# Whole-block stores with x in token order, and an earlier first cast of k, in a linear-attention and MLP kernel

## The chip, the cores and the metric

One core of a Trainium2 chip runs the whole program. The metric is the device time of one execution in microseconds; the median of several runs counts. The engines are TensorE (PE in the profile, with its weight loads as PEld), VectorE (DVE), ScalarE (ACT), GpSimd (POOL) and SyncE (SP), which here only issues transfers.

## The reference

A decayed linear attention over 4 batches, 8 heads, 768 tokens and a head size of 64, in blocks of 64 tokens with a carried state, and then an MLP with a sigmoid-approximated GELU (512 to 2048 to 512) on the 3072 tokens:

```python
for b in range(nb):
    intra = einsum('bhic,bhjc->bhij', qb, kb) * Dmask        # lam**(i-j) for i >= j
    intra = einsum('bhij,bhjd->bhid', intra, vb)
    inter = einsum('bhid,bhde->bhie', qb * lam_pow, kv_state)
    out[:, :, sl] = intra + inter
    kv_state = lam_block * kv_state + einsum('bhsd,bhse->bhde', kb * rev_pow, vb)
x = out.transpose(0, 2, 1, 3).reshape(B * S, H * D)          # 3072 x 512
h = x @ w_in
g = h * (1.0 / (1.0 + exp(-1.702 * h)))
return g @ w_out                                             # 3072 x 512, float32
```

## The kernel before

The 3072 tokens are worked in six waves of 512 (`NW` = 6, `W` = 512). A wave has an attention part, which leaves x turned, features on partitions and tokens on columns, in the tile `xT[w]` (128 x 4 x 512, bf16), and an MLP part. The attention of wave w + 1 is threaded through the MLP of wave w.

**Waves 0 and 1** (`w < ND`) take 256 successive tokens of each of two batches. Half `c` of such a wave is one batch. The loads (L84) put two successive tokens on each partition, so within a block of 128 tokens the attention works with the even tokens first and the odd ones after. `d_out` leaves two PSUM tiles for a half, and `d_x` (L328, called with `i` = 0 and 1) copies each of them, 128 x 512 in f32, to 128 columns of `xT` as bf16. Column a * 64 + s of the block is then token 2s + a. Four such copies are made in each of the two waves: in `end` by ScalarE and VectorE (L756, L757), for the first half of wave 0 both by ScalarE. The order of the columns is carried through the MLP to the partitions of the output block, so a block of 128 tokens goes out in two stores, the even tokens from partitions 0 to 63 and the odd ones from 64 to 127. For wave 1 they stand in `after_product` (L492 to L494), for wave 0 in `leave0` (L536 to L539), which keeps them in `late[n]` for SyncE to issue later (L846, L847, L855, L856). Each store carries two such blocks of tokens (`0:2`) and 256 output columns.

**Waves 2 to 5** take 128 tokens of all four batches. The loads of k, q and v (L88) come in two halves each, over batches. `do_cast` (L196) multiplies a half of k or q by powers of lam and writes bf16, in two instructions; on these waves GpSimd does it (L212). `turn_dma` (L246) then turns the half by a transposing DMA, issued by SyncE (L248). `kT` has one buffer for each half, `ks` two, the loaded `kf` and `qf` one.

**The MLP** uses a scheme of seven products in place of eight for 2 x 2 blocks in both layers. `x_sums` (L569, four VectorE instructions at L577) and `g_sums` (L436, L444) make the sums on its operand side, `in_product` (L579) the first layer's products and `product` (L451) the second's. The results pass through tiles of one pool (tag `o`, 8 buffers): `h_sb` of the first layer (L604) and `o_sb` of the output blocks (L484). Output block 2, 5, 4 and 3 of a wave follow the products of these numbers.

**The order** is written out by hand: `STEPS[w]` is a string of steps that `one_step` (L618) carries out one by one. `a` to `d` with a digit are first-layer products of the wave's groups, `A` to `D` their GELU, `P` a second-layer product, `S`, `M`, `m` the scores and masks of the next wave's attention, `R` its outputs and the state update (`n_state`, L360, VectorE at L371). `K0`, `K1`, `Q0`, `Q1` are the casts of k's and q's halves on GpSimd, `tk0` to `tq1` their turns; they work on wave w + 1. `Lk` and `Lw` load k and q two waves ahead and v one wave ahead. `X` makes the x sums of the next wave. A `+` ahead of a step counts it to the next wave. `G` is a gate: a one-element copy on GpSimd (`gate_pool`, L681) that reads the last of the x sums, so that the casts behind it begin only when these are made. Each engine carries out its instructions in order, and so does SyncE with the transfers that it issues.

Of the kernel before, what the change touches and what calls it, by code (L numbers as in the profile page):

```python
# [25 lines left out]
def kernel(  # L26
# [13 lines left out]
    nc = tc.nc  # L40
    f32 = mybir.dt.float32
    bf16 = mybir.dt.bfloat16
    B, H, S, D = q.shape
    P = 128
# [3 lines left out]
    G = W // P  # L48
# [3 lines left out]
    FFC = d_ff // P  # L52
# [62 lines left out]
    A, Z = slice(0, 64), slice(64, P)  # L115
# [78 lines left out]
    cast, trans, masked, xT, g_of, h_ps, o_ps, t_ps = {}, {}, {}, {}, {}, {}, {}, {}  # L194
# [132 lines left out]

    def d_x(w, c, i, t, copy):  # L328
        n0 = (2 * c + i) * P
        copy(xT[w][:, :, n0 : n0 + P], t)  # L330

    def n_scores(w, p):
        s2 = [acc("ps_s") for _ in range(2)]
# [65 lines left out]
    def mlp1(w, fc):  # L399
        if w not in g_of:  # L400
            g_of[w] = gp.tile([P, FFC, W], bf16, tag="g", name="g_sb")
        j, i = w_in_of[fc]
        h = acc("ps_h", shape=[P, W], tag="mm")
        for kc in range(KC):
            nc.tensor.matmul(h, w_in_sb[j][:, kc, i * P : (i + 1) * P], xT[w][:, kc, :],
                             start=(kc == 0), stop=(kc == KC - 1))
        nc.scalar.activation(g_of[w][:, fc, :], h, GELU)
# [13 lines left out]
    half_sum, blocks, part, c11, c12 = {}, {}, {}, {}, {}  # L421
# [52 lines left out]
    def after_product(w, n, bank, t):  # L474
        if n in (1, 6, 7):
            part[w, n, t.start] = op.tile([P, 2, 256], f32, tag="part", bufs=6, name="part")
            nc.scalar.copy(part[w, n, t.start][:, t], bank[:, t])
            if (w, 4, t.start) in c12:
                after_product(w, 4, c12.pop((w, 4, t.start)), t)
            return  # L480
        if n == 4 and (w, 6, t.start) not in part:
            c12[w, 4, t.start] = bank
            return
        o = op.tile([P, 2, 256], f32, tag="o", name="o_sb")  # L484
        if n == 3:
            nc.scalar.copy(o[:, t], bank[:, t])
        else:
            nc.vector.tensor_tensor(o[:, t], part[w, {2: 1, 5: 7, 4: 6}[n], t.start][:, t], bank[:, t], op=ADD)
        i, c = {2: (0, 0), 3: (0, 1), 4: (1, 0), 5: (1, 1)}[n]
        cols = slice(256 * c, 256 * c + 256)  # L490
        if w < ND:
            rows5 = out.rearrange("(b t s a) d -> a b s t d", t=S // P, s=64, a=2)  # L492
            for a, rows in enumerate((A, Z)):
                nc.sync.dma_start(out=rows5[a, 2 * w + i, :, 0:2, cols], in_=o[rows])  # L494
        else:
            nc.sync.dma_start(
                out=out.rearrange("(b s) d -> s b d", s=S)[w * P : (w + 1) * P, 2 * i + t.start : 2 * i + t.stop, cols],
                in_=o[:, t])
# [19 lines left out]
    def leave0(n):  # L518
        bank = blocks[0, BANK0[int(n)]]
        if n in (1, 6, 7):  # L520
            part[0, n] = op.tile([P, 2, 256], f32, tag="part", bufs=6, name="part")
            nc.scalar.copy(part[0, n], bank)
            return
        if n == 4.5:
            nc.gpsimd.tensor_tensor(o21[0], o21[0], part[0, 7], op=ADD)
            return
        o = op.tile([P, 2, 256], f32, tag="o", name="o_sb")
        if n == 3:
            nc.scalar.copy(o, bank)
        else:  # L530
            nc.vector.tensor_tensor(o, part[0, {2: 1, 5: 7, 4: 6}[n]], bank, op=ADD)
        if n == 4:
            o21.append(o)
        i, c = {2: (0, 0), 3: (0, 1), 4: (1, 0), 5: (1, 1)}[n]

        def store():  # L536
            rows5 = out.rearrange("(b t s a) d -> a b s t d", t=S // P, s=64, a=2)
            for a, rows in enumerate((A, Z)):
                nc.sync.dma_start(out=rows5[a, i, :, 0:2, 256 * c : 256 * c + 256], in_=o[rows])  # L539
        late[n] = store  # L540

    GR = {w: (1, 2, 0, 3) if w > 1 else (1, 2, 3) for w in range(1, NW)}
# [15 lines left out]
    def in_sums(g, which=(0, 1, 2, 3)):  # L558
        t1, t2, t3, t4 = TI[g]
        b11, b12, b21, b22 = (in_pair(g, kh, j) for kh in range(2) for j in range(2))  # L560
        ops = ((t1, b12, b11), (t2, b22, t1), (t3, b22, b12), (t4, b21, t2))
        for i in which:
            o, x, y = ops[i]
            nc.vector.tensor_tensor(o, x, y, op=SUB)

    def x_half(w, i, kh):
        return xT[w][:, 2 * kh : 2 * kh + 2, 256 * i : 256 * i + 256]

    def x_sums(w, which=(0, 1, 2, 3)):  # L569
        if w not in x_sum:  # L570
            x_sum[w] = [xp.tile([P, 2, 256], bf16, tag=f"xs{n}", bufs=1, name="x_s") for n in range(4)]
        s1, s2, s3, s4 = x_sum[w]
        a11, a12, a21, a22 = (x_half(w, i, kh) for i in range(2) for kh in range(2))
        ops = ((s3, a11, a21, SUB), (s1, a21, a22, ADD), (s2, s1, a11, SUB), (s4, a12, s2, SUB))
        for i in which:
            o, x, y, f = ops[i]
            nc.vector.tensor_tensor(o, x, y, op=f)  # L577
# [33 lines left out]
    def in_gelu(w, g, n, bank=None):  # L611
        bank = bank or h_out.pop((w, g, n))
        i, j = {2: (0, 0), 3: (0, 1), 4: (1, 0), 5: (1, 1)}[n]
        a, b = (GROUPS[g][u][j] for u in range(2))
        nc.scalar.activation(g_of[w][:, a : b + 1 : b - a, 256 * i : 256 * i + 256], bank, GELU)  # L615


    def one_step(w, s):  # L618
        if s[0] == "+":
            w, s = w + 1, s[1:]  # L620
        x, a = w + 1, s[1:]
        if s[0] == "f":
            mlp1(w, int(a))
        elif s[0] in "abcd":
            k = "abcd".index(s[0])
            in_product(w, GR[w][k], int(s[1]), TAGS[w][k], dve_copy if s[2:] == "v" else act_copy)
        elif s[0] in "ABCD":
            in_gelu(w, GR[w]["ABCD".index(s[0])], int(a))
        elif s[0] == "i":
            in_sums(0, (int(a),))  # L630
        elif s[0] == "P":
            product(w, int(s[1]), (int(s[2]),))
        elif s[0] in "kq":
            do_cast(x, int(a), s[0], nc.vector)
        elif s[0] in "KQ":
            do_cast(x, int(a), s[0].lower(), nc.gpsimd)
        elif s[0] == "t":
            turn_dma(x, int(s[2]), s[1])
        elif s[0] == "v":
            cast_v(x, int(s[1]), ((act_copy, dve_copy)[s[2:] == "v"],))  # L640
        elif s[0] == "S":
            n_scores(x, int(a))
        elif s[0] == "M":
            n_masks(x, int(a))
        elif s[0] == "m":
            n_masks(x, int(a), True)
        elif s[0] == "R":
            n_rest(x)
        elif s[0] == "o":
            c11.pop(w)()  # L650
        elif s[0] == "X":
            x_sums(x)
        elif s[0] == "G":
            gate_pool(x_sum[w][3][0:1, 0, 0:1])
        elif s[0] == "g":
            m0, m1 = {"l": (0, 4), "h": (4, 8)}[s[1]]
            g_sums(w, m0, m1, tuple(int(c) - 1 for c in s[2:]))
        elif s[0] == "L":
            load(w + (1 if a == "w" else 2), "kq" if a == "k" else "v")
        else:  # L660
            raise ValueError(s)

    STEPS = {
# [17 lines left out]
    def gate_pool(x):  # L681
        nc.gpsimd.tensor_copy(behind_q, x)  # L682
# [209 lines left out]
```

## Time and profile before

| | |
|---|---|
| median of 3 runs | 193.22 us (192.25 to 193.78) |
| the profiled execution | 193.47 us, of which the span from first to last instruction is 191.8 us |
| granted TensorE clock | 1.00 |
| busy: TensorE, VectorE, ScalarE, GpSimd | 183.5, 154.6, 130.0, 53.8 us |
| moved by DMA | 33.91 MB, a mean of 177 GB/s |

The profile is that of one execution. Busy time is the sum of the instructions' durations on an engine; that of TensorE is partly modelled. The chain is followed back from the last instruction, each step to what released it. Line numbers such as L371 are those of the kernel before.

### The profile page before, as it was taken

How to read it: one execution, taken by the hardware profiler on the slowest of the kernel's cores; microseconds unless marked ns; L12 is line 12 of the kernel's file. 1: busy time of each engine (PE TensorE's matmuls, PEld its weight loads, DVE VectorE, ACT ScalarE, POOL GpSimd, SP SyncE). 2: the span in 40 equal slices, each digit the busy share in tenths (PEclk: the TensorE clock that was granted, in tenths of full speed). 3: DMA queues.
4: the chain of work that ended last, by engine and by line, in shares of the span. 5: the costliest groups of instructions: out<-in, count | busy, mean ns of one | idle time of the engine just before them, and what ended most of it. 6: DMA issues, size and time to landing. Idle time of an engine off the chain costs nothing.

```text
span 191.8 us, 5553 instructions
## 1 busy us (share of the span) xinstructions
PE 183.5 (96%) x2291; PEld 150.7 (79%) x2293; DVE 154.6 (81%) x296; ACT 130.0 (68%) x243; POOL 53.8 (28%) x79
## 2 busy tenths in 40 slices
PE   7779999999999999999999999999999999999993
PEld 2356545898788888888888888888888888888882
DVE  1797689997687899979799879799889797889950
ACT  4858566055869976389878388877388876597711
POOL 5298200029738000096000294000393000000000
PEclk9999999999999999999999999999999999999999
DMA  5999999999996799988899756999365903300113
GB/s 154 322 241 161 199 206 206 277 291 295 258 174 139 162 228 243 241 206 135 190 244 221 228 137 140 226 249 251 104 163 121 208 4 113 109 3 0 53 57 112
DMA packets 89599, 33.91 MB, mean 177 GB/s; under 512 B 67430, under 2 KB 89446, under 8 KB 89574
## 3 DMA queue, kind: packets, MB, share of 16 engines
q1 hardware_dynamic: 84676, 28.84, 61.7%
q0 software_dynamic: 4896, 4.72, 14.9%
q8 instruction: 18, 0.29, 0.7%
q14 instruction: 7, 0.06, 0.1%
q10 hardware_dynamic: 2, 0.00, 0.0%
HBM read 27.26 MB, written 6.29 MB: 175 GB/s over the span
## 4 chain that ended last, share of the span: by engine, by line
PE 79%; DMA 12%; DVE 4%; POOL 2%; SPq 1%; issue 0%; ACT 0%; ACTq 0%
PE ps_X L464 19%; PE ps_hX L596 17%; PE ps_V L464 9%; PE ps_hV L596 9%; DMA w_out<-in_moe_w_out_dram 6%; DMA vf<-in_v_dram 6%; PE ps_Q L464 5%; PE ps_hQ L596 4%; PE ps_X L514 3%; DVE w_out_t L431 2%; PE ps_s L338 2%; PE ps_o L393 2%; PE ps_h L417 2%; DVE g_s L444 2%; POOL w_in L184 1%; PE ps_o L380 1%
## 5 line engine op out<-in xcount | busy, mean ns | idle before, releaser
L615 ACT ACTIVATE g_sb<-h_sb 128x512 bf16<-128x512 f32 x57 | 34.5, 632 | 1.2 <-DVE h_sb L604 1.2
L464 PEld LDWEIGHTS <-g_s 128*128 128x128 bf16 x320 | 30.9, 98 | 4.1
L596 PEld LDWEIGHTS <-w_in_t 128*128 128x128 bf16 x304 | 29.7, 98 | 3.6
L224 ACT COPY part<-ps_hX 128x512 f32<-128x512 f32 x34 | 19.5, 586 | 10.4 <-PE ps_hX L596 10.3
L464 PEld LDWEIGHTS <-g_sb 128*128 128x128 bf16 x240 | 22.8, 98 | 3.4
L596 PEld LDWEIGHTS <-w_in 128*128 128x128 bf16 x228 | 22.1, 98 | 2.8
L596 PE MATMUL ps_hX<-x_s,w_in_t 128*128 128x256 bf16 x152 | 22.5, 272 | 0.0
L444 DVE TENSOR_TENSOR g_s<-g_sb 128x1024 bf16<-128x1024 bf16 (+1 forms) x26 | 16.5, 646 | 5.5 <-ACT g_sb L615 5.5
L464 PE MATMUL ps_X<-w_out_t,g_s 128*128 128x256 bf16 x160 | 19.1, 273 | 0.0
L682 POOL CAST behind_q<-x_s 1x1 f32<-1x1 bf16 x4 | 0.7, 174 | 62.2 <-DVE x_s L577 62.2
L212 POOL TENSOR_TENSOR qs<-qf,q_pow 128x512 bf16<-128x512 f32 x16 | 16.3, 1040 | 0.9 <-PE ps_o L301 0.9
L212 POOL TENSOR_TENSOR ks<-kf,k_pow 128x512 bf16<-128x512 f32 x16 | 16.3, 1039 | 0.1
L604 DVE TENSOR_TENSOR h_sb<-part,ps_hX 128x512 f32<-128x512 f32 x19 | 12.9, 681 | 3.9 <-PE ps_hX L596 3.9
L221 DVE COPY part<-ps_hV 128x512 f32<-128x512 f32 x18 | 12.4, 687 | 3.2 <-PE ps_hV L596 3.2
L604 DVE TENSOR_TENSOR h_sb<-part,ps_hV 128x512 f32<-128x512 f32 x19 | 13.0, 684 | 1.0 <-PE ps_hV L596 1.0
L604 DVE TENSOR_TENSOR h_sb<-part,ps_hQ 128x512 f32<-128x512 f32 x19 | 12.9, 681 | 0.4 <-PE ps_hQ L596 0.4
L615 ACT ACTIVATE g_sb<-ps_hX 128x512 bf16<-128x512 f32 x19 | 11.1, 588 | 1.9 <-PE ps_hX L596 1.9
L347 ACT ACTIVATE sm<-ps_s,inv_pow 128x512 bf16<-128x512 f32 x16 | 10.2, 691 | 2.5 <-PE ps_s L338 2.5
L224 ACT CAST v_sb<-vf 128x1024 bf16<-128x1024 f32 (+1 forms) x12 | 10.4, 906 | 1.6 <-DMA vf<-in_v_dram 1.6
L596 PE MATMUL ps_hQ<-xT,w_in 128*128 128x256 bf16 x76 | 11.4, 273 | 0.0
L596 PE MATMUL ps_hV<-x_s,w_in_t 128*128 128x256 bf16 x76 | 11.4, 273 | 0.0
L596 PE MATMUL ps_hV<-xT,w_in_t 128*128 128x256 bf16 x76 | 11.4, 273 | 0.0
(128 smaller groups left out, 364.4 us busy)
## 6 DMA issues: line engine op xcount, KB each, us to landing
kf<-in_k_dram SPq DMA_DIRECT2D x10, 512.0 KB, 6.3
qf<-in_q_dram SPq DMA_DIRECT2D x10, 512.0 KB, 6.7
vf<-in_v_dram SPq DMA_DIRECT2D x10, 512.0 KB, 5.9
out_dram<-o_sb SPq DMA_DIRECT2D x24, 128.0 KB, 2.4
out_dram<-o_sb SPq DMA_DIRECT2D x12, 256.0 KB, 2.6
w_out<-in_moe_w_out_dram POOLq DMA_DIRECT2D x4, 512.0 KB, 14.8
kf<-in_k_dram SPq DMA_DIRECT2D x4, 256.0 KB, 3.1
qf<-in_q_dram SPq DMA_DIRECT2D x4, 256.0 KB, 4.6
```

Of the source, the lines that this page charges most:

```text
L212: eng.tensor_tensor(x.rearrange("p b (r i j d) -> p j (b r) i d", i=2, j=2, d=D)[:, j], f.rearrange("p h (a d) -> p (h a) d", a=2).rearran ...
L221: nc.vector.tensor_copy(out, in_)
L224: nc.scalar.copy(out, in_)
L338: nc.tensor.matmul(s2[h][:, b, :], kT[hs, (b % 2) * NP + p, :], qT[hs, (b % 2) * NP + p, :], start=True, stop=True)
L347: nc.scalar.activation(sm, s, COPY, scale=inv_pow[:, n : n + 1])
L393: nc.tensor.matmul(ps_o[cs, b, :], vt[:, b, 2 * p + i, :], masked[w, 2 * R + i, j][:, b, :], start=False, stop=True, skip_group_check=True)
L444: nc.vector.tensor_tensor(o, x, y, op=f)
L464: nc.tensor.matmul(bank[:, t], x[:, m, t * P : (t + 1) * P], y, start=(n in (1, 2, 7) and t == ts[0] * last and m == 0), stop=(m == FFC // ...
L514: nc.tensor.matmul(bank[:, t], x[:, m, t * P : (t + 1) * P], y, start=(n in (1, 2, 7, 4) and t == 0 and m == 0), stop=(m == FFC // 2 - 1), ...
L596: nc.tensor.matmul(bank[:, u], z[:, kc], y[:, kc], start=(n in (1, 2, 7) and u + kc == 0), stop=(kc == 1), skip_group_check=True)
L604: nc.vector.tensor_tensor(h, h_part[w, g, {2: 1, 5: 7, 4: 6}[n]], bank, op=ADD)
L615: nc.scalar.activation(g_of[w][:, a : b + 1 : b - a, 256 * i : 256 * i + 256], bank, GELU)
```

## The change

There are three edits.

`d_x` writes each PSUM tile to `xT` with the even and odd tokens interleaved, so that the columns of a block stand in token order. The destination steps over every second element; the source is read as before.

With this the output blocks of waves 0 and 1 have token p of the block on partition p, and each is stored in one transfer of 128 partitions: 256 KB in place of two times 128 KB.

In `STEPS` of waves 1, 2 and 3 the steps `K0 tk0` of the following string (the first half of k for waves 3, 4 and 5) move ahead, from behind the gate `G` to a place behind `R`, ahead of the products 5 and 3 and their stores. They get a gate of their own, `H`, which reads the last element of the fourth of the g sums. `G` stays where it was and is now followed, on GpSimd, by `K1`.

```diff
     def d_x(w, c, i, t, copy):
         n0 = (2 * c + i) * P
-        copy(xT[w][:, :, n0 : n0 + P], t)
+        copy(xT[w][:, :, n0 : n0 + P].rearrange("p r (s a) -> p r a s", a=2), t.rearrange("p r (a s) -> p r a s", a=2))
...
         if w < ND:
-            rows5 = out.rearrange("(b t s a) d -> a b s t d", t=S // P, s=64, a=2)
-            for a, rows in enumerate((A, Z)):
-                nc.sync.dma_start(out=rows5[a, 2 * w + i, :, 0:2, cols], in_=o[rows])
+            nc.sync.dma_start(out=out.rearrange("(b t s) d -> b s t d", t=S // P, s=P)[2 * w + i, :, 0:2, cols], in_=o)
...
         def store():
-            rows5 = out.rearrange("(b t s a) d -> a b s t d", t=S // P, s=64, a=2)
-            for a, rows in enumerate((A, Z)):
-                nc.sync.dma_start(out=rows5[a, i, :, 0:2, 256 * c : 256 * c + 256], in_=o[rows])
+            nc.sync.dma_start(out=out.rearrange("(b t s) d -> b s t d", t=S // P, s=P)[i, :, 0:2, 256 * c : 256 * c + 256], in_=o)
...
+        elif s[0] == "H":
+            gate_pool(half_sum[w][3][0:1, FFC // 2 - 1, 0:1])
         elif s[0] == "G":
             gate_pool(x_sum[w][3][0:1, 0, 0:1])
...
     STEPS = {
         1: ("a6 b7 ...
-            "... P60 gl4 gh4 P61 R P50 P51 +a1 X +a2 P30 P31 "),
+            "... P60 gl4 gh4 P61 R H +K0 +tk0 P50 P51 +a1 X +a2 P30 P31 "),
-        2: ("a7v a6 G K0 tk0 b1 b7v A2 ...
+        2: ("a7v a6 G b1 b7v A2 ...
-            "... P60 gl4 gh4 P61 R P50 P51 +a1 X +a2 P30 P31 "),
+            "... P60 gl4 gh4 P61 R H +K0 +tk0 P50 P51 +a1 X +a2 P30 P31 "),
-        3: (as 2)
+        3: (as 2)
-        4: ("a7v a6 G K0 tk0 b1 b7v A2 ...
+        4: ("a7v a6 G b1 b7v A2 ...
```

12 rows, old and new, of the table STEPS are left out of this document.

## The prediction

> **What bounds the kernel now.** I read the page's busy table and its chain first, then the waits of the tensor engine, a table by stage, and last the timelines of VectorE, GpSimd and SyncE around the end of wave 1.
>
> From the page: the busy shares, and the chain by engine.
>
> ```profile
> PE 183.5 (96%) x2291; PEld 150.7 (79%) x2293; DVE 154.6 (81%) x296; ACT 130.0 (68%) x243; POOL 53.8 (28%) x79
> ...
> PE 79%; DMA 12%; DVE 4%; POOL 2%; SPq 1%; issue 0%; ACT 0%; ACTq 0%
> ```
>
> The table by stage (us, busy us and instruction counts of each engine, clock, DMA share, GB/s):
>
> ```profile
> 0.00:15.50 15.50, 11.27 (x185) 6.05 (x187) 9.78 (x23) 9.84 (x24) 8.66 (x25) 1.00 0.88 225
> 15.50:46.00 30.50, 29.73 (x327) 21.11 (x325) 24.77 (x59) 16.58 (x31) 8.92 (x15) 1.00 1.18 239
> 46.00:78.67 32.67, 32.67 (x525) 27.41 (x523) 27.67 (x52) 25.18 (x46) 11.59 (x14) 1.00 0.98 208
> 78.67:106.70 28.03, 28.03 (x354) 24.51 (x353) 24.62 (x44) 20.91 (x37) 8.22 (x9) 1.00 0.95 207
> 106.70:134.74 28.04, 28.04 (x355) 24.52 (x353) 24.63 (x44) 20.91 (x37) 8.22 (x9) 1.00 0.82 203
> ```
>
> TensorE is busy without a gap from 46 us on, at a granted clock of 1.00; asked for its waits between 46 and 188 us, the trace lists none. Waves 2 and 3 take 28.03 and 28.04 us. So the end is set by a stream of matmuls with the same instructions before and after. An edit can gain only where TensorE idles: 4.2 us up to 15.5, 0.8 us up to 46, and 3.3 us in the last stage, where nothing is edited. It loses where it makes an operand late by more than its slack.
>
> **Part 1, x in token order.** Eight copies from PSUM (L330) now write every second bf16 element; source, count and sizes stay. Their rows, five on ScalarE and three on VectorE:
>
> ```profile
> L224 ACT CAST xT<-ps_o x5: 585/592/592, 12.7 to 54.2; 128x512 bf16<-128x512 f32 x5
> L221 DVE CAST xT<-ps_o x3: 691/691/692, 18.6 to 54.4; 128x512 bf16<-128x512 f32 x3
> ```
>
> No row of this trace writes 2-byte elements with a gap. The lower bound is no change; a gain is excluded, since nothing is left out. For the upper bound I double the part that grows with the elements: ScalarE's 256-column copy took 372 ns and the 512-column one 586, so 428 ns of 586 grow; VectorE's forms took 420 and 684, so 528 grow. An upper bound is thus +0.43 us on ScalarE and +0.53 on VectorE. I take 0: the rows run at about 1 ns an element, one element at a time, and a gap changes neither count nor width. What if the upper bound holds? In wave 0, d_x(0,1,1) ends at 19.25, and the matmuls that read it are the second eight of the 24 that begin at 18.50, so near 19.4: 0.4 us late, much of it taken back by the 0.35 us wait for w_in at 22.2. In wave 1, the VectorE copy of 48.38 would end at 49.60 against matmuls at 49.38 (0.2 late), and that of 54.35 at 55.57 against 55.10 (0.5 late). Together 0.7 to 1.1 us.
>
> The Trainium skill ("SBUF — State Buffer", Door 1, the note on cachelines) says that striding costs nothing while two or more successive accesses fall in one 16-byte line; a gap of 4 bytes puts four there, so by it the price is 0. No run here shows it yet.
>
> **Part 2, stores.** Sixteen stores of 64 partitions (L494, L539) become eight of 128, with the same bytes and the same 1 KB pieces. SyncE's issue rows:
>
> ```profile
> L494 SPq DMA_DIRECT2D out_dram<-o_sb x8: 595/605/2718, 77.0 to 83.7; - x8
> L539 SPq DMA_DIRECT2D out_dram<-o_sb x8: 596/606/2478, 50.4 to 69.2; - x8
> 107.46 0.37 SPq L496 DMA_DIRECT2D out_dram<-o_sb  x1
> ```
>
> The last line is a whole 128-partition block of wave 2. So a block costs 0.37 us of SyncE's queue in place of 2 x 0.60: 0.83 saved, 6.6 us over eight blocks. All of it lies beside TensorE, which waits for none of these stores; the loads and turns behind them start sooner. Worth 0 on the path. Had a full store the dearer issue of a half one, 0.60, it would still be 0.
>
> **Part 3, the first k cast and its turn, three times.** Moved: a gate (GpSimd, 0.17 us), two casts of 1.04 us, one transposing DMA (1.23 us of SyncE). Added is the gate H only; G stays. The end of wave 1, VectorE:
>
> ```profile
> 75.14 1.29 DVE L444 TENSOR_TENSOR g_s<-g_sb,g_s 128x1024 bf16<-128x1024 bf16 x2
> 76.34 0.68 DVE L488 TENSOR_TENSOR o_sb<-part,ps_V 128x512 f32<-128x512 f32 x1
> 76.94 1.65 DVE L371 SCALAR_TENSOR_TENSOR kv<-kv,blk_pow,ps_kv 128x256 bf16<-128x256 bf16 x4
> 78.70 0.69 DVE L488 TENSOR_TENSOR o_sb<-part,ps_X 128x512 f32<-128x512 f32 x1
> 79.31 0.75 DVE L577 TENSOR_TENSOR x_s<-xT 128x512 bf16<-128x512 bf16 x2
> ```
>
> and GpSimd as it is now:
>
> ```profile
> 81.11 0.17 POOL L682 CAST behind_q<-x_s 1x1 f32<-1x1 bf16 x1 [19.03 <-DVE x_s L577]
> 81.25 4.06 POOL L212 TENSOR_TENSOR ks<-kf,k_pow 128x512 bf16<-128x512 f32 x4
> ```
>
> H opens when the last of g_s is written, at 76.43. The casts run from about 76.6 to 78.7, in a time when GpSimd sits idle (19.03 us before the gate), and end 0.6 us before the x sums of 79.31. They need k of wave 3: its first load was issued at 69.88 and the median landing of that stage is 5.4 us, so 75.3, and 1.7 us sooner with two late blocks stored faster ahead of it. In the next wave GpSimd then begins k's second half at 81.25 and is done with q 2.08 us sooner, near 87.3 in place of 89.3. The scores that need the turns come at 94.39, and the last turn was issued at 90.29 with landings of 2.7 to 4.6 us in the trace: its margin was small, but no wait is listed, so this is worth 0 here.
>
> What stands behind the new waits: on GpSimd behind H only the casts and G. On SyncE behind the turn stand the stores of blocks 5 and 3. Block 5's sum is ready at 79.4, block 3's copy at 82.0; the turn can go at 78.7. If it holds block 5 back, the next user of that buffer counts: the pool has 8, and the eighth allocation later is the sum of product b4, at 88.38. The store lands 2.4 us after its issue, so it may be issued as late as 86.0, against 79.9 now. Worth 0, with 6 us to spare.
>
> Does a GpSimd cast slow VectorE? One row says yes for one kind of operation: the q cast of 11.83, with both inputs in SBUF, took 1.11 us against a median of 0.42, while four casts ran on GpSimd until 12.64. Sums with one input in PSUM did not suffer: L604 between 83.74 and 85.6 took 0.68 each with GpSimd busy. L371 reads one tensor in SBUF and one in PSUM, like L604, so I take 0. From above: held until the casts end it would run 1.76 us late.
>
> The Trainium skill ("GPSIMD Engine Reference", Key points) names VectorE instructions with two SBUF inputs as those that contend with GpSimd; the 1.11 us agrees, and by it the x sums are in danger and L371 is not, so the sum stays 0 while the casts end by 79.31.
>
> **The sum** is 0 + 0 + 0. The profiled execution took 193.47 us (span 191.8 and 1.7 around it); the median of the three times shown is 193.22. I forecast no change, 193.2.
>
> **Rivals.** (a) *GpSimd holds VectorE up*, slower. Place: L371 under the moved casts, then the x sums. Price: the first sum products of the next wave start at 81.19 (a7, needs the sum ready at 79.73) and 81.62 (a6, needs the one ready at 80.52). So up to 1.10 us of delay is covered, and that is the point from which it decides; 1.76 costs 0.66 us a wave, three times 2.0: 195.2. A late k load is another way to it: casts that begin after 78.3 end past 80.4, into the x sums. For: 11.83's row. Against: L604's rows, and the 0.6 us gap. (b) *Gapped writes are slow*: 0.7 to 1.1 us, 193.9 to 194.3. For: no row shows such a write. Against: one element at a time. (c) *A small gain*: in executions other than the profiled one q's last turn of wave 2 lands late. With 4.6 us from 90.29 it lands at 94.9, 0.5 after the scores begin; once per execution that gives back 0.5: 192.7. (d) *A gain of over 1%*: TensorE would have to lose 1.9 us of its idle time at start and end, which no edit touches, or the start itself to vary: about 191.
>
> **How the numbers follow.** Forecast 0.64; (a) 0.14; (b) 0.09; (c) 0.08; (d) 0.05. One per cent, 1.9 us, is about what a measurement of this kernel can tell from no change: its three times lie 0.8% apart. (a) counts as slower, and of (b) a third, for the case that the writes cost more than twice: 0.17. (d) is faster: 0.05. The rest, 0.78, is within. The range goes from 192.0 (the lowest time before, 192.25, less half of (c)) to 195.2 (case a).
>
> **What would show it.** Right: eight stores of 256 KB, about 0.4 us of issue each; the casts between the g sums and the x sums; L371 at 478 ns and L577 at 420; xT copies at 592 and 691 ns; waves 2 and 3 at 28.0 us. Wrong: waits of TensorE for x_s or xT after 46 us, x sums that wait or take over 0.5 us, waves of 28.7, or copies of xT near 1 us.

## The result and the profile after

The changed kernel takes 193.62 us in the median of 22 runs, the kernel before 192.73 us in 22 runs beside it: a ratio of 1.0054, 95% interval 1.0037 to 1.0072. It is slower by about 1.0 us. The forecast was no change. The time lies inside the range that was given, but the difference is clear of the noise, and it came about in a way that the prediction does not name. Six of the 22 runs had a granted clock of 0.99 and took 194.5 to 195.5 us, and the other kernels have such runs too, so a few tenths of a microsecond between two medians mean little.

The page after, busy shares and chain by engine:

```profile
PE 184.0 (96%) x2293; PEld 151.3 (79%) x2293; DVE 154.7 (81%) x296; ACT 130.6 (68%) x243; POOL 54.2 (28%) x82
...
PE 91%; DVE 3%; DMA 3%; SPq 1%; issue 0%; ACT 0%; DVEq 0%; ACTq 0%
```

The table by stage after, with the columns of the one before:

```profile
0.00:15.50 15.50, 12.19 (x188) 6.65 (x189) 10.06 (x24) 10.33 (x25) 8.94 (x26) 1.00 0.90 228
15.50:46.00 30.50, 29.82 (x327) 21.34 (x325) 25.06 (x60) 17.04 (x31) 10.03 (x17) 1.00 1.20 246
46.00:78.67 32.67, 32.09 (x520) 27.12 (x519) 27.21 (x52) 24.81 (x45) 12.18 (x14) 1.00 0.88 204
78.67:106.70 28.03, 28.03 (x354) 24.51 (x353) 24.62 (x44) 20.91 (x37) 8.44 (x11) 1.00 0.95 216
106.70:134.74 28.04, 28.04 (x354) 24.51 (x353) 24.62 (x44) 20.92 (x37) 8.40 (x11) 1.00 0.82 191
```

Waves 2 and 3 still take 28.03 and 28.04 us, with TensorE busy throughout. The stage of wave 1, which had no gap, now has 0.58 us of idle TensorE. The two profiled executions have the same span, 191.8 us, but in the one before TensorE idled 0.92 us more up to 15.5 us (busy 11.27 us there, 12.19 after), so what the change costs can't be read from their spans. The waits of TensorE after name the place (engine, line, awaited: us in total, times, longest):

```profile
PE ps_hQ L592 <- DVE xT L221: 0.6, 1, 0.6
PE ps_h L417 <- DVE xT L221: 0.5, 1, 0.5
```

Both are new, and both are for the xT copy on VectorE. (`ps_h` and `ps_hQ` are the PSUM tiles that the waiting matmuls write; in the kernel before, L592 is L596.) The two places in TensorE's timeline after:

```profile
18.29 0.28 PE L417 MATMUL ps_h<-xT,w_in 128*128 128x256 bf16 x1
19.08 2.69 PE L417 MATMUL ps_h<-xT,w_in 128*128 128x256 bf16 x23 [0.51 <-DVE xT L221]
...
54.65 0.61 PE L592 MATMUL ps_hQ<-xT,w_in 128*128 128x256 bf16 x4 [0.57 <-DVE xT L221]
```

and the same two in the kernel before:

```profile
18.50 2.79 PE L417 MATMUL ps_h<-xT,w_in 128*128 128x256 bf16 x24
...
54.49 0.61 PE L596 MATMUL ps_hQ<-xT,w_in 128*128 128x256 bf16 x4
```

Before, 24 matmuls run without a stop. After, one runs, and the other 23 wait for VectorE. But the first eight of these matmuls read columns 0 to 255 of `xT`, and the copy that they wait for, `d_x(0,1,1)`, writes columns 384 to 511. Likewise in wave 1, where product b2 (hQ) reads columns 0 to 255 and waits for `d_x(1,1,1)`. They wait for data that they don't read. The 0.51 us that the trace lists is less than the delay: the first matmul counts as busy until 18.57, while the second could have followed it after 0.11 us, at 18.40, and came at 19.08, so 0.68 us late.

The program's own list of instructions with their waits says the same. For wave 0, these are the instructions that carry a wait (number in TensorE's order of weight loads and matmuls, line):

```text
before   528 L417 Ldweights w_in_143 [waits for the w_in transfer]
         544 L417 Ldweights w_in_142 [waits for VectorE]     first reader of columns 256 to 511
after    528 L417 Ldweights w_in_143 [waits for the w_in transfer]
         530 L417 Ldweights w_in_143 [waits for VectorE]     second matmul on columns 0 to 255
wave 1   before 1440 (L417, columns 256 to 511), after 1432 (hQ, columns 0 to 255)
```

An `Ldweights` is the weight load that goes ahead of its matmul. The wait on ScalarE, for the other copy of the same half, moves along in both waves, to the matmul behind the weight load named. Nowhere else in TensorE's list does a wait on an engine differ between the two kernels.

The positions fit one reading. `xT` is 4 rows of 512 columns on each partition; a copy into columns 384 to 511 of each row, taken as one span from its first to its last element, covers 384 to 2047. Row 0's columns 0 to 255 lie outside it, and the first matmul reads row 0 and is free; the second reads row 1 and waits. b2 begins with row 2 and waits at once. So the gapped write seems to be ordered by its span, where the plain one was ordered exactly. The positions of the waits are shown; that the span is the rule behind them is drawn from the positions.

The copies themselves, and for the third part GpSimd and VectorE at the end of wave 1:

```profile
L224 ACT CAST xT<-ps_o x5: 728/737/741, 12.5 to 53.8; 128x512 bf16<-128x512 f32 x5
L221 DVE CAST xT<-ps_o x3: 726/727/732, 18.3 to 53.9; 128x512 bf16<-128x512 f32 x3
```

```profile
76.55 0.17 POOL L680 CAST behind_q<-g_s 1x1 f32<-1x1 bf16 x1 [14.64 <-DVE g_s L444]
76.69 2.05 POOL L212 TENSOR_TENSOR ks<-kf,k_pow 128x512 bf16<-128x512 f32 x2
81.18 0.18 POOL L680 CAST behind_q<-x_s 1x1 f32<-1x1 bf16 x1 [2.44 <-DVE x_s L573]
81.31 2.05 POOL L212 TENSOR_TENSOR ks<-kf,k_pow 128x512 bf16<-128x512 f32 x2
83.33 4.06 POOL L212 TENSOR_TENSOR qs<-qf,q_pow 128x512 bf16<-128x512 f32 x4
```

```profile
76.93 1.65 DVE L371 SCALAR_TENSOR_TENSOR kv<-kv,blk_pow,ps_kv 128x256 bf16<-128x256 bf16 x4
79.30 0.76 DVE L573 TENSOR_TENSOR x_s<-xT 128x512 bf16<-128x512 bf16 x2
```

Eight copies are slower, by 145 ns on ScalarE and 36 ns on VectorE. The moved casts end at 78.74, 0.56 us ahead of the x sums, and L371 takes 1.65 us as before. And the stores of the two waves (least/median/most ns of issue):

```profile
L492 SPq DMA_DIRECT2D out_dram<-o_sb x4: 372/474/2605, 76.4 to 82.0; - x4
L535 SPq DMA_DIRECT2D out_dram<-o_sb x4: 462/1276/2552, 49.5 to 67.7; - x4
```

### The profile page after: what moved, and what is told of

The parts are those of the page before. It is cut to its first block, busy times and chain, and to the rows that moved or that the text cites. A ratio compares the mean times of both kernels' runs of the same rounds, so it can differ in the third digit from the quotient of the medians.

```text
span 191.8 us, 5550 instructions
## 1 busy us (share of the span) xinstructions
PE 184.0 (96%) x2293; PEld 151.3 (79%) x2293; DVE 154.7 (81%) x296; ACT 130.6 (68%) x243; POOL 54.2 (28%) x82
## 4 chain that ended last, share of the span: by engine, by line
PE 91%; DVE 3%; DMA 3%; SPq 1%; issue 0%; ACT 0%; DVEq 0%; ACTq 0%
PE ps_X L464 19%; PE ps_hX L592 17%; PE ps_V L464 9%; PE ps_hV L592 9%; PE ps_h L405 5%; PE ps_Q L464 5%; PE ps_hQ L592 4%; PE ps_h L417 4%; PE ps_X L512 4%; DMA qf<-in_q_dram 3%; PE ps_s L338 2%; PE ps_o L393 2%; PE ps_t L241 2%; DVE sm L270 1%; PE ps_s L262 1%; PE ps_o L380 1%
## 5 line engine op out<-in xcount | busy, mean ns | idle before, releaser
L592 PEld LDWEIGHTS <-w_in_t 128*128 128x128 bf16 x304 | 29.7, 98 | 3.6
L224 ACT COPY part<-ps_hX 128x512 f32<-128x512 f32 x34 | 19.5, 587 | 10.4 <-PE ps_hX L592 10.2
L592 PEld LDWEIGHTS <-w_in 128*128 128x128 bf16 x228 | 22.1, 98 | 3.4 <-DVE xT L221 0.7
L592 PE MATMUL ps_hX<-x_s,w_in_t 128*128 128x256 bf16 x152 | 22.5, 272 | 0.0
L680 POOL CAST behind_q<-g_s 1x1 f32<-1x1 bf16 x3 | 0.5, 175 | 48.9 <-DVE g_s L444 48.9
L592 PE MATMUL ps_hQ<-xT,w_in 128*128 128x256 bf16 x76 | 11.4, 273 | 0.6 <-DVE xT L221 0.6
L347 ACT ACTIVATE sm<-ps_s,inv_pow 128x512 bf16<-128x512 f32 x16 | 10.2, 691 | 2.5 <-PE ps_s L338 2.5
L592 PE MATMUL ps_hV<-x_s,w_in_t 128*128 128x256 bf16 x76 | 11.4, 273 | 0.0
L592 PE MATMUL ps_hV<-xT,w_in_t 128*128 128x256 bf16 x76 | 11.4, 273 | 0.0
L592 PE MATMUL ps_hX<-x_s,w_in 128*128 128x256 bf16 x76 | 11.3, 272 | 0.0
```

Source lines behind the costliest of these rows:

```text
L224: nc.scalar.copy(out, in_)
L347: nc.scalar.activation(sm, s, COPY, scale=inv_pow[:, n : n + 1])
L592: nc.tensor.matmul(bank[:, u], z[:, kc], y[:, kc], start=(n in (1, 2, 7) and u + kc == 0), stop=(kc == 1), skip_group_check=True)
```

## The experiments

Three theories stood after the result. **W**: the widened wait costs the time. **S**: the slower copies cost it. **K**: the moved cast and turn cost it. A fourth, that the whole stores cost it, had no run of its own; the runs with whole stores and no wait answer it (last section of the experiments). Ratios are to the kernel before, run beside each on the same chip.

### The parts by themselves

Token order and whole stores, with the steps of the kernel before (the edit is the change less all of `STEPS` and `H`):

> The change without its third part: token order and whole stores, the steps of the kernel before. Theory W (the gapped write makes the first matmuls on columns 0 to 255 wait for the copy of columns 384 to 511): slower than before by 0.5 to 1.1 us (ratio 1.003 to 1.006), with two waits of TensorE for xT near 18.6 and 54.1 us, 0.5 and 0.6 us, as in the changed kernel. Theory K (the moved cast and turn cost the time): ratio 0.998 to 1.002. Theory S (the copies are slower, 737 and 727 ns, and that is all): also 1.003 to 1.006, but for another reason, which the third run separates.

Measured: 193.71 us, ratio 1.0054 (1.0021 to 1.0086), with waits for xT of 0.4 and 0.6 us. The loss is there without the third part.

The third part alone:

```diff
-        2: ("a7v a6 G K0 tk0 b1 ... P61 R P50 ...
+        2: ("a7v a6 G b1 ... P61 R H +K0 +tk0 P50 ...
```

> The kernel before with the third part alone: H, K0 and tk0 moved in waves 1 to 3. Theories W and S: ratio 0.998 to 1.002, no wait of TensorE for xT, waves 2 and 3 at 28.03 us each, L371 at 478 ns. Theory K: ratio 1.003 to 1.006, with a longer wave or a new wait after 76 us.

Measured: 193.02 us, ratio 1.0005 (0.9975 to 1.0035), no wait for xT, L371 at 472 ns. One wait after 76 us is there, 0.23 us up to 93.51 us for a turn of q, which theories W and S did not expect:

```profile
93.51 0.51 PE L338 MATMUL ps_s<-qT,kT 64*128 64x128 bf16 x12 [0.23 <-DMA qT<-qs]
```

The changed kernel lists no such wait. K falls as the cause of the loss, though the interval does not rule out a few tenths of a microsecond.

### The same gap without the widened wait

```diff
-            xT[w] = xp.tile([P, NP, W], bf16, tag="x", name="xT")
+            xT[w] = xp.tile([P, 2, NP, W // 2] if w in SPLIT else [P, NP, W], bf16, tag="x", name="xT")
...
-        copy(xT[w][:, :, n0 : n0 + P].rearrange("p r (s a) -> p r a s", a=2), ...)
+        y = xT[w][:, c, :, i * P : i * P + P] if w in SPLIT else xT[w][:, :, n0 : n0 + P]
+        copy(y.rearrange("p r (s a) -> p r a s", a=2), ...)
```

with `SPLIT = (0, 1)`, and the readers of `xT` taking the half as the outer index.

> The changed kernel, with xT of waves 0 and 1 laid out as two halves of 256 columns one behind the other, so that a copy into the second half spans none of the first. Same copies, same gap of 4 bytes, same instructions. Theory W: the two waits for xT go, copies stay near 737 and 727 ns, and the time is that of the kernel before, ratio 0.998 to 1.002. Theory S: the copies are as slow, so the ratio stays at 1.003 to 1.006.

Measured: 192.54 us, ratio 0.9982 (0.9954 to 1.0009). TensorE's waits hold none for xT, while the copies are as slow as in the changed kernel:

```profile
L225 ACT CAST xT<-ps_o x5: 734/737/744, 12.2 to 53.0; 128x512 bf16<-128x512 f32 x5
L222 DVE CAST xT<-ps_o x3: 730/731/733, 18.0 to 53.1; 128x512 bf16<-128x512 f32 x3
```

S falls: the loss goes with the wait and not with the copies. In this kernel's list every wait of TensorE on an engine stands where it stood in the kernel before, while the copies have their gap. In TensorE's timeline the eight matmuls of columns 256 to 511 in wave 1 follow b2 within 0.05 us:

```profile
53.24 0.61 PE L597 MATMUL ps_hQ<-xT,w_in 128*128 128x256 bf16 x4
53.90 1.05 PE L420 MATMUL ps_h<-xT,w_in 128*128 128x256 bf16 x8
```

### The same wait without the gap

```diff
-        for c, a in ((0, 2), (1, 0), (1, 2)):
+        for c, a in ((1, 0), (0, 2), (1, 2)):
             mlp1_half(0, c, a, a + 1)
...
+        mlp1_half(1, 1, 14, 15)
         one_step(1, "b2")
         state()
         x_sums(1, (1, 2, 3))
-        mlp1_half(1, 1, 14, 15)
```

> The kernel before, with plain copies and split stores, in which the matmuls that truly need the last copy of xT are put first: in wave 0 the half on columns 256 to 511 ahead of that on 0 to 255, in wave 1 likewise ahead of product b2. It has the waits without the gap. Theory W: 0.5 to 1.2 us slower (1.003 to 1.006), two waits for xT of 0.5 to 0.8 us, copies at 592 and 691 ns. Theory S: ratio 0.998 to 1.002.

Measured: 194.11 us, ratio 1.0076 (1.0044 to 1.0108), above W's expectation: 1.5 us where 0.5 to 1.2 were expected. The waits are there, in wave 0 at the very first matmul and so longer than in the changed kernel:

```profile
19.29 2.79 PE L417 MATMUL ps_h<-xT,w_in 128*128 128x256 bf16 x24 [0.86 <-DVE xT L221]
...
55.12 1.05 PE L417 MATMUL ps_h<-xT,w_in 128*128 128x256 bf16 x8 [0.54 <-DVE xT L221]
```

The copies take 592 and 691 ns here. So plain copies, too, cost time when their first reader comes early: 1.5 us for 1.40 us of these waits and another of 0.2 us for an x sum, where the changed kernel lost 1.0 us with 1.08 us of waits. The edit also moves other work of wave 1 by eight matmuls, so the last tenths are not accounted for.

### Wave by wave

The two-halves layout in wave 0 alone (`SPLIT = (0,)`), and in wave 1 alone (`SPLIT = (1,)`):

> The changed kernel with the two-halves layout of xT in wave 0 alone. Theory W: one wait for xT is left, about 0.6 us near 54 us, none near 18.6; ratio to before 1.001 to 1.004.

> The same layout in wave 1 alone. Theory W: one wait for xT is left, 0.4 to 0.5 us near 18.6 us, none near 54. What follows it up to 46 us may give part back, since the kernel before waited there for weights, 0.35 and 0.26 us; ratio to before 0.999 to 1.003.

Measured: with wave 0 laid out in halves 193.38 us, ratio 1.0038 (1.0011 to 1.0065), one wait for xT of 0.6 us left; with wave 1 laid out in halves 193.17 us, ratio 1.0024 (1.0008 to 1.0041). Of 192.7 us these are 0.7 us for wave 1's wait (0.2 to 1.3) and 0.5 us for wave 0's (0.2 to 0.8); together 1.2 against the 1.0 of the whole change, inside their intervals. The expectation for wave 0's wait failed in the profiled execution of `e6_halves_w1`: it shows 0.68 us of waiting for a load of w_in there and none for xT:

```profile
18.91 2.90 PE L420 MATMUL ps_h<-xT,w_in 128*128 128x256 bf16 x24 [0.68 <-DMA w_in<-in_moe_w_in_dram]
```

That load comes at a different time in each execution, and where it is late it hides the wait for the copy.

### What makes the copy dearer

```diff
-        copy(xT[w][:, :, n0 : n0 + P], t)
+        copy(xT[w][:, :, n0 : n0 + P].rearrange("p r (a s) -> p a r s", a=2), t.rearrange("p r (a s) -> p a r s", a=2))
```

> The kernel before, whose xT copies walk the same columns in eight runs of 64 elements without a gap, in place of four of 128. It tells what makes a copy dearer: if it is the gap, 592 and 691 ns as before; if it is the number of runs, near 737 and 727. No early wait for xT.

Measured, one execution: 192.42 us, copies at 591 and 691 ns, and no wait for xT. The gap makes the copy dearer, not the eight runs; and in this program's list, too, the wait on VectorE stays at number 544.

### Are stores and moved cast worth anything?

> The two-halves layout with token order and whole stores, and the steps of the kernel before: no third part. If the moved cast and turn are worth nothing, the same as with them, ratio to before 0.996 to 1.001. If they gain, it is slower than with them by 0.2 us or more.

Measured: 192.97 us, ratio 1.0007 (0.9986 to 1.0029). This was on another chip than the two-halves kernel with the third part, so that one and this one were run again side by side, with the changed kernel:

> The changed kernel as it is, beside the next two on one chip. Ratio to before 1.003 to 1.007, with the two waits for xT.

> The changed kernel with the two-halves layout of xT in waves 0 and 1, a second time, to tell whether it beats the kernel before. Theory W alone: 0.997 to 1.001. A true gain from stores and moved cast: under 0.999 with its whole interval.

> The two-halves layout without the third part, a second time. If the moved cast and turn are worth nothing, within 0.2% of the run before this one.

Measured: the changed kernel 193.50 us, ratio 1.0043 (1.0021 to 1.0064); with two halves 193.04 us, 1.0006 (0.9981 to 1.0032); with two halves and without the third part 192.89 us, 1.0014 (0.9987 to 1.0040). The two-halves kernel undoes the loss but does not beat the kernel before: its first ratio, 0.9982, was not repeated. Whole stores are in all of these two-halves kernels, so they cost nothing that can be told either. No version here is faster than the kernel before by more than the noise. The profiled executions of all three wait for w_in ahead of the first matmuls of wave 0, 0.64, 0.80 and 0.96 us. In that of the changed kernel this hides the wait for xT in wave 0, so of the two waits that were expected it shows one, 0.57 us in wave 1.

## Why the prediction was wrong, point by point

**What bounds the kernel** was right, and so was the rule drawn from it: an edit loses where it makes an operand late by more than its slack. The loss came in just that way. The forecast of no change was wrong all the same, and it was by luck that the range held the time: it reached up to 195.2 for rival (a), which did not happen.

**Part 1 is the step that failed.** It priced the copy and gave it 0, and it put the copy's first reader at "the second eight of the 24", near 19.4, and at the matmuls of 55.10. These are the readers that need the data. In the changed program the first to wait are the second matmul of the first eight, which could go at about 18.4, and b2, which could go at 54.08 (54.65 less its wait). The edit widened what the copy is ordered against, and that took away 0.77 us of cover in wave 0 (seven matmuls of 0.11) and 0.44 us in wave 1 (four). The prediction had no term for this: it held the waits fixed and varied only durations, and what it put at 0 is 1.0 us. Its upper bound of 0.7 to 1.1 us has the same size by chance, since it came from copies longer by 0.43 and 0.53 us.

The copy's price, too, was off, though inside the bounds: +145 ns on ScalarE and +36 on VectorE, where 0 was taken and 430 and 530 were the ceiling. `e3_halves` shows that this alone costs nothing that can be measured.

The Trainium skill ("SBUF — State Buffer", Door 1, the note on cachelines) has such a stride free up to eight bf16 elements; the trace differs, 592 to 737 ns on ScalarE for a step of two, and the measurement decides.

**Part 2** was right on the path and in its least row: 372 ns for a whole block where a half took 595. Its sum of 6.6 us of queue time was too high: the groups of stores take 15.5 us of SyncE's timeline before and 10.2 us after, 5.3 us less, with medians of 474 and 1276 ns and single issues of up to 2605. TensorE waits for none of them.

**Part 3** was right in its price and nearly throughout: casts from 76.69 to 78.74 (forecast 76.6 to 78.7), q done at 87.39 (87.3), L371 and the x sums undisturbed, ratio 1.0005 alone. The turn went at 79.64 and not at 78.7, behind two stores that held the queue from 76.42 to 79.54.

**Rivals.** (a), GpSimd holding VectorE up, did not happen, and the row that spoke for it, 11.83, is of an operation with both inputs in SBUF, which L371 is not. (b), gapped writes, came closest: it named the right copies, and 0.7 to 1.1 us; but it put the lateness at the matmuls that need the data, and would have got there by copies of 1.0 to 1.2 us, and these take 0.73 to 0.74. As a mechanism it is refuted by `e3_halves`. (c) did not show: TensorE waited 0.23 us for q's turn, up to 93.51, in the profiled execution of `e2_k_only`, with the cast already moved. (d) did not come. The line "what would show it wrong" did name waits of TensorE for xT.

## What to carry to other kernels

Before an edit to the destination pattern of a copy is priced, ask which readers are ordered behind it, not only which ones need its data: a write with a gap may be ordered as one span, and then a matmul on columns that it never touches waits for it. When parts of a tile are filled at different times, lay the tile out so that the span of a late write does not cross what is read early; here a change of layout took two waits of half a microsecond away at no cost that could be measured. Where the bounding engine has no gaps, look for the first instruction that carries a wait on the edited one, before and after: here it had moved in just two places, and that can be read without a run.

## What was not expected of the hardware

A write of 512 bf16 elements from PSUM with a step of two elements takes ScalarE 737 ns against 592 without it, and VectorE 727 against 691 (a partition's share of a 128x512 copy); eight runs of 64 without a gap take the same as four runs of 128 (591 and 691). And the load of w_in that the first matmuls of wave 0 need lands at times that differ between executions: the profiles show no wait for it (`e2_k_only`, where these matmuls began at 17.80 us) or one of up to 0.96 us (`e11_halves_nok_again`, at 19.67 us), so part of what is lost in that place is lost anyway.
